# A new order of steps behind the start of the MLP, in a kernel of a DeltaNet block and an MLP block on one core

## The chip, the cores and the metric

The kernel runs on one core of one Trainium2 chip. The metric is the device time of one execution in microseconds (us); smaller is better. A run of the kernel before gave 519.6 us as the median of three (516.92 to 520.19).

The engines are named as in the profile: PE is TensorE (PEld its weight loads), DVE is VectorE, ACT is ScalarE, POOL is GpSimd and SP is SyncE, which here only issues DMAs. Each engine runs its instructions strictly in its own program order, and waits on semaphores for what other engines make.

## The reference, cut to what matters

The first block is the delta rule, a linear attention with a state of 48 x 48 for each of 4 x 8 heads, over 768 positions. The second is a layer norm without bias, two matrix products with a ReLU between them, and a residual.

```python
k_n = k / (np.linalg.norm(k, axis=-1, keepdims=True) + 1e-06)
for t in range(S):
    kt, vt, bt = (k_n[:, :, t], v[:, :, t], beta[:, :, t, None])
    y[:, :, t] = np.einsum('bhd,bhde->bhe', q[:, :, t], state)
    v_old = np.einsum('bhde,bhd->bhe', state, kt)
    state = state + bt[:, :, :, None] * np.einsum('bhd,bhe->bhde', kt, vt - v_old)
...
x = np.ascontiguousarray(attn_out.transpose(0, 2, 1, 3)).reshape(B, S, H * D)
xn = (x - mu) / np.sqrt(var + 1e-06) * g_ln
ch = np.maximum(xn @ w_ch1, 0.0) @ w_ch2
return (x + ch).astype(np.float32)
```

All is float32: q, k, v are (4, 8, 768, 48), w_ch1 is 384 x 1536 and w_ch2 is 1536 x 384.

## The kernel before, in words

**The recurrence in chunks.** The 768 positions are cut into 12 chunks of 64. Within a chunk the recurrence becomes products of matrices. For chunk c the steps have these names, which the later text uses:

- G (line 822): the gram product of the keys, 64 small matmuls ("a block"); ACT copies it to SBUF and SP sends it to DRAM and back in another layout.
- The inverse of a triangular matrix. For pairs of chunks `rows_inverse` (tags x1 to x5) does it row by row on DVE: 31 pairs of a product into `tmp` (line 910) and a subtraction from `xb` (line 917). Two short products e and z (lines 984 and 990) join the halves; chunk 1 has an extra pair (lines 947 and 952) around it.
- P (line 822, with the queries), ks and qs (line 1036, keys and queries against the state), u (lines 1055 and 1060 for chunk 1, line 1091 later), s (line 1108, the change of the state, which DVE adds to `s_all` in line 1118), y (line 1098, the chunk's output). Each is a block of 64 matmuls of 48 to 64 rows and columns.
- Between ks and u, DVE subtracts from v (line 1043). Behind y, ACT copies to `x`, DVE and ACT do the layer norm (lines 1142 to 1154), and the result is turned: by PE for the first three chunks (line 1188), by DVE and five DMAs on SP later (lines 1165 and following).

**The MLP by chunks.** `mlp(c)` runs for each chunk's 256 tokens. Chunk 0 has its own form (m0: first products in line 1410, second products in line 1452). Later chunks use a form of the second product with seven in place of eight block products (line 1527), whose combinations POOL makes (lines 1514 and 1552); from chunk 3 on the first product has fifteen block products (line 1311) with sums on POOL, DVE and ACT (lines 1271, 1294, 1334, 1329, 1338). Chunks 1 and 2 use line 1430.

**The weights** come as 64-bit words and are turned to float32 by a short chain for each of twelve pieces: ACT (lines 587 and 595), DVE (line 592), POOL (line 605).

**Keys and queries** of later chunks come into three buffers `tb` by eight DMAs each (`load_blocks`), the keys' from POOL's queue and the queries' from SP's, all issued in line 404; DVE turns each in one instruction (line 802).

**What sets the order.** Each piece of work is added to a list as a step with an engine, a function and the steps it depends on: 3,037 in all, numbered as they are added. `Line.emit` then runs the functions in the order that the string ORDER gives (numbers, ranges, and `f` for a filler matmul that keeps PE busy). So ORDER sets each engine's program order. `in_this_order` fixes it with dependencies that need no semaphore, and also ties the order of the DMAs of SP and ACT to each other. The synchronisation by data is put in by the framework, whatever the order is, with one exception in `emit`: a POOL step that is no DMA gets a semaphore wait for the last DVE step marked `port` that stands ahead of it in ORDER:

```python
if s.eng == "DVE" and s.plan.get("port"):
    shared = made[-1]
if s.eng == "Pool" and "bulk" not in s.plan and shared is not seen:
    tc.add_manual_dep(made[n], shared.name, ..., reason="shared port")
```

ORDER is written out by hand in the file; the costs that the steps carry (`dve(n)`, `act(n)`, `PASS`, due times in `DUE` and `CAP`) are not used when the kernel is built.

**Steps that the later text names**, with their numbers in ORDER:

| steps | what |
|---|---|
| 418, 420, 421 | chunk 1: the product of line 952 (`z` of its join), DVE's transpose of line 973, e1 |
| 437, 439, 438, 426 | chunk 1: ks1, DVE's subtraction from v, qs1, z1 |
| 440, 441, 443, 444, 445 | chunk 1: u in two halves, s1, DVE's sum into `s_all`, y1 |
| 480, 481 | x1: two small steps, on DVE and on POOL |
| 483 to 544 | x1: the 62 DVE instructions of its inverse |
| 658 to 665, 666, 667 | chunk 4: eight loads of keys from POOL's queue, DVE's turn (kt), G4 |
| 670 to 677, 678, 679 | chunk 5: the same, G5 |
| 375, 377; 381, 383; 387, 389; 393, 395 | pieces of w_ch2: DVE's conversion (line 592) and POOL's (line 605) |
| 396 | POOL: a memset ahead of loads of x1 |
| 572 to 617 | m0: first products on PE and ReLUs on ACT |
| 618 to 646 | m0: the last first product (618) and the second products |
| 787 to 795, 796 | chunk 2: loads of queries on SP, DVE's turn, P2 |
| 803, 805, 562 | s2, y2, e3 |
| 814, 867 | chunk 2: DVE's normalisation (line 1154); chunk 1's MLP: a combination on POOL (line 1514) |
| 924, 2140 | a load of keys on SP, for chunk 3 and for chunk 8 |
| 1199, 1201 | s4, y4 |

## Time and profile before

| what | value |
|---|---|
| time, median of three runs | 519.6 us (516.92 to 520.19) |
| span of the profiled execution, first to last instruction | 514.1 us |
| what the median has beyond that span | 5.5 us |
| PE busy | 493.1 us, 96% of the span |
| DVE busy | 353.5 us, 69% |
| POOL busy | 284.8 us, 55% |
| ACT busy | 206.9 us, 40% |
| granted PE clock | 0.999 of full speed |
| DMA, 16 queues, mean over the span | 106 GB/s |

The profile is of one execution, and gives its span; a device time of that same execution is not among the numbers, so the 5.5 us also hold what executions differ by. Busy times of PE are made of pipelined matmuls whose ends are modelled; the distance from one start to the next is the safer measure, and a step's "usual distance" below is its median over the steps of the same kind. A product of line 1527 is one matmul call and shows as two MATMUL records (the float32 passes), one of line 1311 as four, a block as 64. "issue" in the waits view is time in which an engine waited for nothing that the profile shows.

In the slices of the page PE is busy for nine tenths or more from the sixth slice on (about 64 us); before that, in the start that the change leaves as it is, PE waits more.

### The profile page before, as it was taken

To read this page: it belongs to the slowest core of one execution; us is meant where nothing else is said; L and a number is where in the kernel's file an instruction comes from. 1 tells how busy PE (TensorE), PEld (TensorE's weight loads), DVE (VectorE), ACT (ScalarE), POOL (GpSimd) and SP (SyncE) were. 2 spreads that over 40 slices of the span, in tenths; PEclk is the share of its full clock that TensorE was granted. 3 is DMA by queue.
4 is the path that set the end of the run, shared out by engine and by line. 5 is a ranking of instruction groups with operands and counts; after the bars stand their busy time and mean duration, and the time that the engine had idled before them with its cause. 6 is when DMAs were issued, how large, how long until landed. Compare 5 with 4: busy or idle time off the path is not lost.

```text
span 514.1 us, 22905 instructions
## 1 busy us (share of the span) xinstructions
PE 493.1 (96%) x10022; PEld 450.7 (88%) x10022; DVE 353.5 (69%) x816; ACT 206.9 (40%) x462; POOL 284.8 (55%) x447
## 2 busy tenths in 40 slices
PE   5897899999999999999999999999999999999997
PEld 3675797668888898999999999999999999999996
DVE  4688479899994999975997847898727346254241
ACT  4785764422533333351434343423514425324140
POOL 2634583144658879749477465283274551844644
PEclk9999999999999999999999999999999999999999
DMA  8958895577338755387454474313660321202011
GB/s 207 251 83 192 221 191 127 128 173 117 67 60 207 123 117 92 73 221 123 80 108 62 105 203 76 99 15 53 132 149 12 88 36 41 57 13 82 8 24 31
DMA packets 181635, 54.56 MB, mean 106 GB/s; under 512 B 164888, under 2 KB 177312, under 8 KB 181536
## 3 DMA queue, kind: packets, MB, share of 16 engines
q1 hardware_dynamic: 168512, 40.10, 37.4%
q10 hardware_dynamic: 10816, 9.83, 6.3%
q0 software_dynamic: 2208, 3.17, 4.3%
q8 instruction: 78, 1.28, 1.1%
q14 instruction: 21, 0.17, 0.1%
HBM read 36.30 MB, written 16.78 MB: 103 GB/s over the span
## 4 chain that ended last, share of the span: by engine, by line
PE 85%; DVE 5%; DMA 3%; issue 2%; ACT 1%; SPq 1%; POOL 1%; DVEq 0%; ACTq 0%; POOLq 0%
PE f L1527 28%; PE f L1311 24%; PE f L1430 6%; PE two L822 3%; PE f L1452 3%; DMA tb<-in_q_dram 2%; PE by L1098 2%; PE by L1036 2%; PE two L1091 2%; PE two L1036 2%; PE two L1108 2%; PE f L1605 1%; DVE xb L917 1%; SPq L404 1%; DMA kr<-in_k_dram 1%
## 5 line engine op out<-in xcount | busy, mean ns | idle before, releaser
L1527 PE MATMUL f<-w_sb,h_all 128*128 128x192 f32 x396 | 83.9, 330 | 0.0
L1514 POOL TENSOR_TENSOR h_all<-h_all 128x256 f32<-128x256 f32 x99 | 74.8, 767 | 9.4 <-PE f L1527 3.3
L1527 PE MATMUL f<-words,h_all 128*128 128x192 f32 x396 | 79.5, 329 | 0.2 <-POOL h_all L1514 0.2
L1552 POOL TENSOR_TENSOR words<-h_all 128x128 f32<-128x128 f32 x66 | 30.2, 478 | 74.4 <-ACT h_all L1338 50.2
L1334 DVE TENSOR_TENSOR h_all<-f,h_all 128x512 f32<-128x512 f32 x72 | 49.2, 686 | 30.5 <-PE f L1311 25.9
L1527 PEld LDWEIGHTS f<-w_sb,h_all 128*128 128x128 f32 x396 | 65.3, 190 | 1.6 <-POOL h_all L1514 0.2
L1527 PEld LDWEIGHTS f<-words,h_all 128*128 128x128 f32 x396 | 65.1, 190 | 1.6 <-POOL h_all L1514 1.0
L910 DVE TENSOR_TENSOR tmp<-xb,gb 128x31 f32<-128x31 f32 (+19 forms) x139 | 56.0, 403 | 3.7 <-POOL xb L897 0.5
L917 DVE TENSOR_TENSOR xb<-xb,tmp 128x31 f32<-128x31 f32 (+19 forms) x139 | 51.4, 370 | 2.5
L1329 ACT COPY h_all<-f 128x512 f32<-128x512 f32 x45 | 25.8, 586 | 62.9 <-PE f L1311 39.3
L404 POOL DMA_DIRECT2D tb<-in_k_dram x64 | 41.9, 658 | 8.2 <-PE f L631 7.1
L1338 ACT ACTIVATE h_all<-h_all 128x512 f32<-128x512 f32 x54 | 32.5, 626 | 30.0 <-DVE h_all L1334 29.8
L1311 PE MATMUL f<-x_new,w_sb 128*128 128x128 f32 x288 | 41.4, 278 | 0.0
L1311 PE MATMUL f<-xnt,w_sb 128*128 128x128 f32 x288 | 40.4, 278 | 0.1
L1311 PEld LDWEIGHTS f<-x_new,w_sb 128*128 128x128 f32 x288 | 37.4, 191 | 0.4
L1311 PEld LDWEIGHTS f<-xnt,w_sb 128*128 128x128 f32 x288 | 36.8, 191 | 0.5 <-issue 0.2
L1430 PE MATMUL f<-xnt,w_sb 128*128 128x256 f32 x144 | 33.9, 383 | 0.0
L1430 PEld LDWEIGHTS f<-xnt,w_sb 128*128 128x128 f32 x144 | 26.7, 190 | 3.5
L605 POOL TENSOR_TENSOR w_sb<-words 128x768 uint32<-128x768 uint32 (+1 forms) x11 | 15.3, 1400 | 23.7 <-issue 18.2
L1545 DVE TENSOR_TENSOR o<-f,x 128x192 f32<-128x192 f32 x33 | 11.2, 348 | 24.9 <-PE f L1527 17.2
L1136 ACT COPY x<-by 128x384 f32<-128x384 f32 x23 | 10.6, 481 | 42.6 <-DVE o L1545 27.2
L1527 PE MATMUL f<-w_sb,words 128*128 128x192 f32 x132 | 27.6, 332 | 0.0
(247 smaller groups left out, 1003.6 us busy)
## 6 DMA issues: line engine op xcount, KB each, us to landing
words<-in_moe_w_ch_dram ACTq DMA_DIRECT2D x20, 384.0 KB, 5.2
gd<-gsb SPq DMA_DIRECT2D x11, 512.0 KB, 4.1
v<-in_v_dram SPq DMA_DIRECT2D x24, 192.0 KB, 3.6
kr<-in_k_dram SPq DMA_DIRECT2D x46, 96.0 KB, 3.7
out_dram<-o SPq DMA_DIRECT2D x46, 96.0 KB, 2.5
xld<-xlt SPq DMA_DIRECT2D x9, 384.0 KB, 3.6
xnt<-xld SPq DMA_DIRECT2D x36, 96.0 KB, 3.0
tb<-in_q_dram SPq DMA_DIRECT2D x40, 64.0 KB, 3.5
```

The source lines that it names most:

```text
L404: add(eng, cost, lambda: QUEUE[eng].dma_start(out=out_, in_=in_), r, w, bulk=n * ns / 16e3, np=n, **kw)
L910: lambda j=j, n=n, w=w, t=t: nc.vector.tensor_tensor(out=t, in0=xv[:, 0:n, j : j + 1].to_broadcast([128, n, w]), in1=gv[:, j : j + 1, j + ...
L917: "DVE", dve(n * w), lambda t=t, rest=rest: nc.vector.tensor_tensor(out=rest, in0=rest, in1=t, op=ALU.subtract),
L1036: nc.tensor.matmul(dst[half(e), hp, j], src[drows(hp), (e if n else key_half(c, hp, e)) * GP + j], s_all[drows(hp), e, j], start=(n == 0 o ...
L1311: nc.tensor.matmul(wide(p[:, f : f + 128]), w[:, f : f + 128], r, start=start and i == 0, stop=True, skip_group_check=True)
L1329: add("ACT", act(512), lambda: nc.scalar.copy(o, p), pk, ok)
L1334: add("DVE", dve(512), lambda: nc.vector.tensor_tensor(out=o, in0=x, in1=y, op=op), [*xk_, *yk], ok)
L1338: add("ACT", act(512), lambda: nc.scalar.activation(o, o, ACTF.Relu, scale=scale), [], ok)
L1430: nc.tensor.matmul(p[:, 0:TOK], w1_sb[:, t, f * 128 : (f + 1) * 128], xnt[:, t], start=(t == 0), stop=(t == KC - 1))
L1514: add(eng, cost, lambda: e.tensor_tensor(out=out_, in0=x, in1=y, op=op), r, w, port=2 if eng == "Pool" else 1, pr=-2)
L1527: lambda f=f, t=start and f == order[0]: nc.tensor.matmul(p[:, 0:D2], lhs(f), rhs[:, f], start=t, stop=(f == order[-1]), skip_group_check=True
L1552: lambda f=f + i: e.tensor_tensor(out=s3[f], in0=one(0, 0)[0](f), in1=one(1, 0)[0](f), op=ALU.subtract),
```

## The change

Only the string ORDER changes (lines 131 to 248). The first 374 of its entries stay; the next 2,674 are the same steps in another order; the last 14 stay. On PE the first 50 steps are the same, up to s0, the state's first change, at 59.6 us; on DVE the first 128, on ACT 106, on POOL 39 and on SP 44. No step, instruction, buffer or dependency by data changes; the waits marked "shared port" follow from ORDER and so change with it.

The diff, cut to the stretches that the later text speaks of:

```diff
 ORDER = """
...
-250 345 349-350 576 578 406 362 577 579 301 407 321 333 432 431 309 307 302-303 308 304 473 306 305 471-472 474 788
-351 356 363 357 252 658 415 433-434 582 580 598 370 364 581 599 373 435 604 583 605 368 584 610 586 365 413 470 414
-611 585 588 416 372 587 475 590 401 787 790 792 789 791 793-794 589 379 417 591 378 592-596 616 600 374 597 602 601
-606 418 376 603 608 436 666 369 476-479 481-489 480 490-495 375 496-499 670 675 672 1073 674 677 377 371 676 500
-419-420 501 617 607 380 635 609 636 614 391 421 437 502-507 381 508 795 509 439 510-519 424 615 423 612 620 438 384
-390 382 425 422 426 429-430 428 427 637 621 440-441 638 385 392 442 639 445 394 386 447 443 520-523 444 524 393
-525-527 622-623 667 624 640 383 678 387 668 446 388 613 389 679-680 528 450 529 395 1085 625-626 618 530 451 448 455
-531 456 449 452 532 650 533 457 534 453-454 535-536 651 537 641 627 642-643 628-629 644 796 458 462 645 630 538 652
...
-559 711-713 655 714-715 692 716 561 717-728 562 801 863 841 846 802 864 805 854 856 866 927 843 857 855 936 729 565
-564 563 566 865 803 807 806 730 810 808 848-849 809 811 815 812 847 731 804 876-877 869-870 732 813 871 937 567 872
...
+578 576 356 362 359 432 431 306 304-305 303 473 307-308 302 472 474 471 787 363 357 415 579 364 577 252 582 580 598
+433-434 581 368 599 583 370 673 470 365 373 435 604 584 586 605 610 378 416 369 670 371 413-414 587 379 585 588 611
+372 475 417 589-590 924 788-790 792 794 791 793 784 591-594 596 418 595 597 602 600 616 601 603 608 380 376 617 609
+374 436 476-479 674 665 675 481-497 419-420 498-500 381 437 421 606 385 607 614 612 635-636 666 677 672 676 375 377
+423 425 613 422 424 390-391 439 480 678 501-521 426 438 615 620-621 637 429 428 427 622 382 430 440 384 441 623 618
+638-639 442 394 392 443 386 388 445 383 795 1073 393 395 466 444 522-525 387 667 640 446-448 450 449 451 668 452 389
+396 468 624-625 641 679-680 455 619 650 526-527 453 528-529 651 530-531 652 456 532 454 457 533-544 642-643 796
...
+558 557 560 840-841 860 713 655 561 714-722 657 723-731 801 861-863 846 864 843 802 865 467 856 927 857 866 936 805
+803 562 807 565 563 566 806 564 810 808 811 815 809 812 847 804 848-849 732 876-878 567 879 816 733 937 817 813 734
...
 3032-3034 3026 3035 3027 3036
 """
```

PE's part of the first stretch, read out of these lines with the names of the steps (f for a product of m0):

| order | PE from step 418 to G4 |
|---|---|
| before | z, f, f, f, f, e1, ks1, f, f, qs1, z1, f, f, u, u, f, f, y1, s1, f, f, G4 |
| after | z, f, f, f, f, ks1, e1, f, f, f, f, f, z1, qs1, f, f, f, f, u, u, f, f, f, f, s1, y1, G4 |

## The prediction

> **What bounds the kernel now.** I read the page's busy times first, then the waits of TensorE (PE) behind the start of the MLP, then the timeline where they lie.

> ```profile
> span 514.1 us, 22905 instructions
> ...
> PE 493.1 (96%) x10022; PEld 450.7 (88%) x10022; DVE 353.5 (69%) x816; ACT 206.9 (40%) x462; POOL 284.8 (55%) x447
> ...
> q8 instruction: 78, 1.28, 1.1%
> ```

> PE is the bound: 96% of the span. The waits view, PE alone, from 61 us (the new order begins on PE at 61.5 us) to the end, adds up to only 4.2 us:

> ```profile
> PE by L1036 <- issue: 1.3, 1, 1.3
> PE two L822 <- issue: 0.8, 2, 0.6
> PE two L1108 <- issue: 0.7, 1, 0.7
> PE two L1091 <- issue: 0.4, 1, 0.4
> PE two L1055 <- issue: 0.4, 1, 0.4
> PE f L1527 <- POOL h_all L1514: 0.2, 1, 0.2
> PE two L1036 <- issue: 0.2, 1, 0.2
> PE f L990 <- ACT es L996: 0.2, 1, 0.2
> ```

> Nearly all is "issue": PE stopped inside a block of 64 small matmuls and no semaphore ended it. Three of these stops in the timeline of PE:

> ```profile
> 87.02 0.95 PE L1036 MATMUL by<-s_all,qt 48*64 48x48 f32 x49 [1.26 <-issue]
> ...
> 91.03 0.56 PE L1055 MATMUL two<-v,xt 32*64 32x48 f32 x22 [0.36 <-issue]
> ...
> 102.84 0.32 PE L822 MATMUL two<-kt 48*64 48x64 f32 x2 [0.63 <-issue]
> ```

> The windows view counts the PE instructions between these stops:

> ```profile
> 87.02:91.03 4.01, 3.55 (x127) 2.45 (x128) 3.84 (x9) 2.25 (x5) 0.00 (x0) 1.00 0.40 123
> 91.03:102.84 11.81, 10.99 (x384) 7.92 (x383) 9.55 (x20) 5.29 (x8) 2.29 (x2) 1.00 0.54 125
> ```

> 127 + 128 = 255 and 384 + 383 = 767, three times 255.7. The page has 20,044 PE instructions in 78 packets of its instruction queue: 257 each. So the stops sit on packet ends: PE waits there for its next code. A block issues 128 instructions in about 1 us, so two blocks use up a packet in 2 us, while in these lines the next one came 4.01 us later.

> Start to start, the PE steps from 61.5 to the last one at 509.8 us take 448.3 us. Each step's usual distance to the next, summed, is 434.0: some 332 for the products of the MLP (462 of L1527 at 0.325, 270 of L1311 at 0.447, 24 of L1430 at 1.295, 46 of L1410 and L1452 at 0.67 and 0.645) and 102 for the blocks (0.68 to 1.09 each) with their changeovers. Some 76 short pauses of 0.105 make 8; 12 longer stops make 6.1 (5.3 on code, 0.8 on ACT or POOL). Of the 6.1, 3.8 lie between 87 and 104 us. This 6.1 is all that an order can win.

> **The change part by part.** The same 3,037 steps run; none is added or removed. Another step stands ahead of 657 of PE's 957, 460 of DVE's 816, 318 of ACT's 489, 352 of POOL's 443 and 259 of SP's 332.

> *PE's own work.* A changeover from a product to a block costs 0.093 (0.540 against 0.447), back some 0.11. The old order has 68 of each, the new 67. The sum of distances stays 434.0: 0, bounds -0.2 and +0.2.

> *The stretch from the product `z` of chunk 1 (step 418) to the gram block G4 (667).* Here DVE decides. DVE in the groups view, from the end of the transpose L973 (step 420) to the start of the state sum L1118 (step 444):

> ```profile
> L917 DVE TENSOR_TENSOR xb<-xb,tmp 128x240 f32<-128x240 f32 (+6 forms) x11 | 5.7, 517 | 0.3
> L910 DVE TENSOR_TENSOR tmp<-xb,gb 128x231 f32<-128x231 f32 (+6 forms) x12 | 4.9, 406 | 0.3
> L802 DVE STREAM_TRANSPOSE qt<-tb 128x1024 f32<-128x1024 f32 x1 | 1.2, 1239 | 0.0
> L1118 DVE TENSOR_TENSOR s_all<-s_all,two 128x768 f32<-128x768 f32 x1 | 1.0, 955 | 1.9 <-PE two L1108 1.9
> L1043 DVE TENSOR_TENSOR v<-v,two 128x768 f32<-128x768 f32 x1 | 0.9, 944 | 0.0
> L592 DVE TENSOR_SCALAR words<-words 128x768 uint32<-128x768 uint32 x1 | 0.6, 555 | 0.0
> ```

> 26 instructions, 13.3 us, then 1.9 idle for PE. The new order puts 32 there: two more transposes L802 (kt of chunks 4 and 5, steps 666 and 678: 2 x 1.24), two more conversions L592 (2 x 0.555), step 480 (0.2) and one more L917 (0.35): 13.3 + 4.1 = 17.4. PE gets five more products L1410 there (eight for three): its distances from 418 to G4 go from 17.0 to 17.0 + 5 x 0.67 - 0.15 = 20.2. From the start of 418 (78.00) to the end of L973 (81.41) it is 3.4 now. So G4 can start 3.4 + 17.4 + 0.95 (L1118) + 0.3 (now 97.97 - 97.66) = 22.1 behind 418, and PE is there after 20.2: it waits 1.9. With the shortest times of the inverse's 24 instructions it is 0.3, and with PE's two packet ends (below) still open ahead of it up to 3.8. I take 1.9, by the durations of the same instructions. In the old order the stretch and the one behind it cost the 3.8 named above; the new one has no packet used up in under 3.5 us from G4 to the end of the MLP's first chunk, and P2 comes 6.2 behind G4 instead of 10.1. Net -1.9, bounds 0 and -3.5.

> *DMAs and POOL here.* On POOL the loads of `tb` (665, 672 to 677; 0.66 of POOL each, landing after 3.0 to 3.5) now follow each other ahead of the conversion 377, so that kt 678 can stand early on DVE: they are issued behind step 481, some 5 us ahead of need. The memset 396 (0.95) goes from the first place on POOL to behind the conversion 389; its reader is a load near 117 us. On SP the load 924 of chunk 3 goes ahead of the eight loads of chunk 2 (0.62 later), and those of chunk 8 move up to 79 places. Adding SP's issues at 0.62 and the landings of the page's DMA list to each release, the least margin to the PE step served is 5.4 us (5.1 in the old order): 0. If that cover went, each place would cost PE 0.6.

> *Code supply behind 110 us.* From the packet ends found above I counted on, 255 PE instructions at a time. By distances, a packet is used up in under 3.5 us at eight places of the new order, twelve of the old. Behind 110 us the shortfall to 3.5 sums to 4.8 (old: 5.5); the longest are y2, s2, e3 in a row (1.8 us for a packet: 1.7) and y4, s4 (2.1: 1.4). The old order's 5.5 cost a measured 1.5. At that rate the new costs 1.3: -0.2, bounds -1.5 and +3.3 (the full 4.8). [...]

> *Handovers behind 110 us.* PE steps that wait for another engine: with row durations added along each, 16 of 357 have less than 0.15 us of cover in the old order, 26 in the new. The old 16 cost 0.8; 26 at that rate 1.3: +0.5, bounds -0.8 and +2. Adding each queue's instructions from their releases, DVE's worst lag behind its PE reader is 0.6 (old 2.2, at L1118 of chunk 6), POOL's 0.3 (old 0.4).

> *A shared port.* POOL steps wait for the last marked DVE step ahead of them in ORDER: 51 such waits behind the fork for 57. The tightest new one is the combination 867 of chunk 1 behind DVE's 814, with 0.2 us of cover: 0 to +0.5, taken as 0. Queued behind it are the other combinations of that MLP, and PE's products of L1527 wait for them.

> Sum: 0 - 1.9 - 0.2 + 0.5 = -1.6. The profiled span of 514.1 becomes 512.5. The median of the three runs, 519.6, stands 5.5 above the span, which I carry over: 518.0.

> **The rivals.**
> *1. No waits are left.* The order was placed so that all handovers meet: 519.6 - 6.1 = 513.5. For it: DVE's worst lag falls from 2.2 to 0.6. Against: 1.8 us for a packet at y2, s2, e3, and 17.4 us on DVE ahead of G4.
> *2. DVE is held by POOL ahead of G4.* In that stretch POOL runs three conversions L605 (377, 383, 395; mean 1.4 on the page) where the old order had two. If DVE stands still for each, G4 waits 4.2 more: 522.2. It is slower than before from 1.6 more. Against: now POOL is busy for 2.2 us in the stretch and DVE's idle time there, the wait for PE apart, is 0.6. [...]
> *3. Code arrives every 4.0 us all along,* as it did at 87 to 91 us. Then the packets behind 110 us lose 9.6 instead of 1.3: 518.0 + 8.3 = 526.3, slower. It decides from 3.6 us on (over 1% from 3.9). Against: by the same count the old order would have lost 11.6 there and lost 1.5; for: back-to-back blocks y2, s2, e3 are new.

> **How the numbers follow.** Forecast 0.52, rival 1 0.10, rival 2 0.20, rival 3 0.18. The likeliest alone reaches from 516.0 to 521.0. To leave out no more than 2 in 10 the range goes from 514.5 (most of rival 1 out) to 524.0 (rival 2 in, most of rival 3 out). About 1%, 5.2 us, is what a measurement of this kernel can tell from no change (the three runs spread over 516.92 to 520.19). Faster by more, under 514.4: 0.7 of rival 1, 0.07. Slower by more, over 524.8: 0.7 of rival 3 and a little of rival 2, 0.16. The rest, 0.77, is within 1%.

> **What would show it.** Right: PE's waits from 61 us on stay between 2 and 6 us; the 1.3 and 0.6 on "issue" at 87 and 103 us are gone; G4 follows L1118 and waits 1 to 3 us for it, DVE having no idle time ahead. Wrong: a stop of over 1.5 us on "issue" at y2, s2, e3 (near 135 us) or at y4, s4 (rival 3); POOL's L605 and DVE's L910 stretched beside each other ahead of G4 (rival 2); a wait for a DMA landing anywhere on PE (the SP margin was wrong); or a PE sum of distances that is not 434.

## The result, and the profile after

The new order is slower: 524.54 us, median of four runs (522.86 to 526.28), against 518.67 before (four runs, 516.92 to 520.19). The ratio is 1.011, 95% interval 1.008 to 1.015. The forecast was 518.0 with a range of 514.5 to 524.0: wrong in sign, and the median lies outside the range. In the later sessions before ran more often and its median was 516.6 to 516.9, so ratios, each against before's runs of the same session, are what to compare below. The ratios leave out two later executions that lay over 1.5% above the fastest of their kernel (523.28 of "new to 808, then old" and 525.45 of "new, loads spread" in the table of experiments).

The profiled execution of the new order took 522.86 us, span 521.1, against a span of 514.1. From its page:

```profile
span 521.1 us, 22880 instructions
...
PE 498.5 (96%) x10022; PEld 453.9 (87%) x10022; DVE 351.3 (67%) x816; ACT 207.3 (40%) x462; POOL 280.5 (54%) x447
...
PEclk9998998999999999999999999999999999999999
```

PE is the bound as it was, and the span is 7.0 us longer. In the clock row (tenths of full speed) slices 4 and 7 show 8: from 45.6 and from 79.75 us the clock was halved for 3.41 us each (granted 0.50 in both windows). The first lies in the common beginning, the second does not. The waits view of PE from 61 us to the end (line, what it waited for, us in all, times, longest):

```profile
PE by L948 <- issue: 1.6, 1, 1.6
PE f L1307 <- DVE h_all L1330: 0.9, 1, 0.9
PE f L1406 <- ACT h_all L1414: 0.9, 1, 0.9
PE f L1523 <- POOL h_all L1510: 0.7, 1, 0.7
PE by L1094 <- issue: 0.7, 1, 0.7
PE f L986 <- issue: 0.7, 2, 0.4
PE f L980 <- issue: 0.6, 1, 0.6
PE f L1523 <- DVE o L1541: 0.5, 1, 0.5
PE two L1051 <- issue: 0.4, 1, 0.4
PE by L1032 <- ACT xt L998: 0.2, 1, 0.2
```

(Lines are four lower than before's.) It sums to 7.2 us where before had 4.2, and what is new are waits for data: 3.2 us for DVE, ACT and POOL where before had 0.4.

To lay the whole out I use the prediction's measure: each PE step's distance to the next, less the usual distance of its kind. What is above counts as loss: waits, short pauses, and halved clock. I count from s0 (358), PE's last common step, to 832, the second PE step of chunk 1's MLP, and from there to PE's last step. Between two kernels a figure of loss is good to about 0.5:

| one profiled execution each | s0 to 832: usual + loss | 832 to the end: usual + loss |
|---|---|---|
| before | 51.8 + 6.2 | 383.0 + 9.3 |
| after | 50.2 + 8.4 | 384.2 + 14.4 |

The first part costs 0.6 more and the second 6.3 more, nearly all of the difference between the spans. The loss behind 832 grew by 5.1. Of that, waits over 0.13 us make 3.8 (6.1 against 2.3), and within these handovers of data 3.3 (4.1 against 0.8). Three of after's handovers (197.6, 223.6 and 419.0 us) make 2.5 of its 4.1.

Two places in the trace of after show how a part of it comes about. **Late place, 219 us.** DVE, then POOL, in the timeline (start, us, engine, line, operation, tiles, shape):

```profile
219.27 2.29 DVE L906 TENSOR_TENSOR tmp<-xb,gb 128x207 f32<-128x207 f32 x1
221.48 1.23 DVE L798 STREAM_TRANSPOSE kt<-tb 128x1024 f32<-128x1024 f32 x1
222.65 0.33 DVE L913 TENSOR_TENSOR xb<-xb,tmp 128x207 f32<-128x207 f32 x1
222.90 0.68 DVE L1330 TENSOR_TENSOR h_all<-f,h_all 128x512 f32<-128x512 f32 x1
```

```profile
218.91 0.66 POOL L400 DMA_DIRECT2D tb<-in_k_dram  x1
219.58 1.28 POOL L1267 TENSOR_TENSOR w_sb<-w_sb,qt 128x512 f32<-128x512 f32 x1
220.80 0.46 POOL L1290 TENSOR_TENSOR x_new<-x_new,xnt 128x128 f32<-128x128 f32 x1
221.22 0.79 POOL L1541 TENSOR_TENSOR o<-o,words 128x192 f32<-128x192 f32 x1
```

The product into `tmp` (step 1153) takes 2.29 us; in before the same step took 0.37:

```profile
216.59 0.37 DVE L910 TENSOR_TENSOR tmp<-xb,gb 128x207 f32<-128x207 f32 x1
```

In after it starts beside a POOL instruction, POOL's next two follow without a gap, and it ends 0.3 behind the end of L1290. Behind it on DVE stand a turn (1.23) and then L1330 (step 1265), whose input PE had finished at 218.7. PE waits for that sum until 223.63.

**Late place, 415 us.** POOL's timeline:

```profile
411.64 0.73 POOL L1510 TENSOR_TENSOR h_all<-h_all 128x256 f32<-128x256 f32 x1
414.62 1.48 POOL L681 TENSOR_TENSOR v<-v,kpair 128x768 f32<-128x768 f32 x1 [2.25 <-DMA v<-in_v_dram]
416.06 0.73 POOL L1510 TENSOR_TENSOR h_all<-h_all 128x256 f32<-128x256 f32 x1
```

POOL stands 2.25 us for a transfer: step 2720 scales v of chunk 11, and SP's load 2714 that it needs is issued at 410.98. In before it was issued at 381.64, and 2720 waited for nothing:

```profile
418.78 1.48 POOL L685 TENSOR_TENSOR v<-v,kpair 128x768 f32<-128x768 f32 x1
```

Its product is used by DVE at 445.1. The combinations L1510 for the running MLP stand behind it, and PE waits for one of them until 419.03. Six traces have the load at this place (one of them, shown below, carried into before), and PE's wait follows POOL's: POOL stood 1.2, 1.5, 2.3, 3.4, 3.8 and 7.1 us for v, and PE 0, 0, 0.7, 1.9, 2.2 and 6.8 for POOL.

**Early place, 66 to 79 us.** The chain of waits of after:

```profile
66.44 6.06 DMA gb<-gd
...
72.57 0.26 ACT nrm_b L882
72.83 0.49 ACT es L951
73.31 0.18 ACT h_all L1414
73.49 0.04 issue
73.53 2.27 PE f L1406 x18
75.81 0.67 PE by L948 x49
76.47 1.62 issue
```

A load takes 6.06 us to land (the new order issues four weight loads of ACT within 3.3 us there, where before spread them over 7; with the loads spread out, in an experiment below, it landed in 2.8), ACT waits for it, PE waits 0.9 for ACT, then stops 1.62 inside `z` for code, and the halved clock follows. This looked like the main cause. It was not, as the first two experiments show.

### The profile page after: what moved, and what is told of

It reads as the page before. It is cut to its first block, busy times and chain, and to the rows that moved or that the text cites. A ratio compares the mean times of both kernels' runs of the same rounds, so it can differ in the third digit from the quotient of the medians.

```text
span 521.1 us, 22880 instructions
## 1 busy us (share of the span) xinstructions
PE 498.5 (96%) x10022; PEld 453.9 (87%) x10022; DVE 351.3 (67%) x816; ACT 207.3 (40%) x462; POOL 280.5 (54%) x447
## 3 DMA queue, kind: packets, MB, share of 16 engines
q8 instruction: 78, 1.28, 1.0%
## 4 chain that ended last, share of the span: by engine, by line
PE 75%; DVE 6%; DMA 6%; SPq 4%; ACT 4%; issue 3%; POOL 1%; DVEq 0%; ACTq 0%; POOLq 0%
PE f L1523 27%; PE f L1307 20%; SPq L400 4%; PE f L1426 3%; PE two L818 3%; PE f L1448 3%; PE two L1032 2%; PE by L1094 2%; PE f L1406 2%; PE by L1032 2%; PE two L1087 1%; DMA tb<-in_q_dram 1%; DMA gb<-gd 1%; DMA xld<-xlt 1%; ACT xt L728 1%
## 5 line engine op out<-in xcount | busy, mean ns | idle before, releaser
L1510 POOL TENSOR_TENSOR h_all<-h_all 128x256 f32<-128x256 f32 x99 | 73.2, 750 | 19.9 <-PE f L1523 9.8
L1523 PE MATMUL f<-w_sb,h_all 128*128 128x192 f32 x396 | 81.6, 330 | 0.0
L1548 POOL TENSOR_TENSOR words<-h_all 128x128 f32<-128x128 f32 x66 | 29.0, 457 | 78.9 <-ACT h_all L1334 38.6
L1330 DVE TENSOR_TENSOR h_all<-f,h_all 128x512 f32<-128x512 f32 x72 | 49.0, 685 | 30.7 <-PE f L1307 24.2
L1541 DVE TENSOR_TENSOR o<-f,x 128x192 f32<-128x192 f32 x33 | 11.3, 352 | 38.1 <-PE f L1523 28.1
```

The costliest lines, as they stand in the source:

```text
L1330: add("DVE", dve(512), lambda: nc.vector.tensor_tensor(out=o, in0=x, in1=y, op=op), [*xk_, *yk], ok)
L1510: add(eng, cost, lambda: e.tensor_tensor(out=out_, in0=x, in1=y, op=op), r, w, port=2 if eng == "Pool" else 1, pr=-2)
L1523: lambda f=f, t=start and f == order[0]: nc.tensor.matmul(p[:, 0:D2], lhs(f), rhs[:, f], start=t, stop=(f == order[-1]), skip_group_check=True
L1548: lambda f=f + i: e.tensor_tensor(out=s3[f], in0=one(0, 0)[0](f), in1=one(1, 0)[0](f), op=ALU.subtract),
```

## The experiments

Theories at the start: **1**, the early burst of loads; **2**, thinly covered handovers in the later part; from the second group on theory **3**, a special case of 2: a queue works in order, so an instruction that waits for a transfer, or that DVE or POOL holds up for the other, stops all that stands behind it; and **4**, the supply of code. Ratios are against before. Edits of ORDER are shown as the order on one engine's queue.

The losses are of one profiled execution each, which can lie far from its kernel's median: 527.77 for a median of 522.05 in the third row, the slowest of its six.

| kernel | ratio, 95% interval | loss s0 to 832 | loss behind 832 |
|---|---|---|---|
| after | 1.0111 (1.0076 to 1.0146) | 8.4 | 14.4 |
| new to 808, then old | 0.9997 (0.9973 to 1.0020) | 6.4 | 9.3 |
| old to 808, then new | 1.0108 (1.0065 to 1.0152) | 6.3 | 17.0 |
| new, loads spread | 1.0076 (1.0040 to 1.0112) | 5.4 | 14.7 |
| new, nrm_b later | 1.0095 (1.0059 to 1.0131) | 5.8 | 13.8 |
| new, four moves | 1.0071 (1.0041 to 1.0102) | 7.9 | 11.3 |
| before, two moves | 1.0197 (1.0161 to 1.0233) | 6.2 | 19.6 |
| new, packets shifted | 1.0178 (1.0139 to 1.0216) | 8.3 | 12.3 |
| new, ten moves | 1.0047 (1.0015 to 1.0080) | 3.8 | 13.2 |
| new, ten moves, e3 apart | 1.0068 (1.0041 to 1.0095) | 5.5 | 11.7 |
| loads spread, then old | 0.9989 (0.9970 to 1.0008) | 4.8 | 10.9 |
| the same, mended | 0.9976 (0.9947 to 1.0004) | 6.3 | 9.3 |

**Halves exchanged.** The first 808 entries of the one order (to about 120 us), then the remaining steps in the other's sequence.

```diff
-ORDER = new
+ORDER = new[:808] + [s for s in old if s not in new[:808]]
```

> The new order up to its 808th entry (about 120 us, the start of the second chunk's MLP), then all remaining steps in the order of before. In the two profiles PE's stops above usual distance sum to 13.0 us in the new order (7.0 of it from 60 to 104 us, 6.1 behind) against 6.1 (3.8 and 2.3). Theory 1, the early burst of loads: most of the loss arises ahead of 104 us and stays with this kernel: 3 to 4 us over before (ratio 1.006 to 1.008), with ACT's nrm_b waiting over 2 us for gb, a stop on issue of over 1 us near 78 us and a stretch of half clock of 3.4 us behind it. Theory 2, thinly covered handovers in the later part of the new order: this kernel is within 1 us of before (0.998 to 1.002).

```diff
-ORDER = new
+ORDER = old[:808] + [s for s in new if s not in old[:808]]
```

> The order of before up to its 808th entry, then the remaining steps in the new order. Theory 1, the early burst of loads: no wait of ACT for gb over 1 us, no half clock between 60 and 500 us, and only the later part's 3.8 us over before are left or less: ratio 1.002 to 1.007. Theory 2, the later handovers: all of the loss stays: 5 to 6 us over before (1.010 to 1.012). With the kernel above, the two differences against before should sum to about that of the whole new order (5.9 us).

Measured 0.9997 and 1.0108. Theory 1 fell: with the new beginning alone the time is before's, although its trace has the same stop (1.89 us near 78 us): it loses 6.4 us ahead of 832 where before loses 6.2. All of the slowdown comes with the later part, whose loss is 9.3 with the old sequence and 14 to 17 with the new; and the two differences sum to 1.05% where the whole new order has 1.11%. One point of theory 1's failed too: the clock was halved behind 420 us in the second kernel's trace (mean granted 0.990), which it had excluded.

**Loads spread, and ACT's step later.** In the first, of the queues of ACT and SP, 378, 379 and 401, 784, 924 go back:

```diff
-ACT: 378 ... 379 585 ... 589      SP: 401 early, 784 and 924 with the loads of m0
+ACT: 585 ... 589 379 591 378      SP: 401 behind 788, 784 and 924 ahead of 785
```

> The new order with five loads spread out as before had them: two of ACT's four weight loads issued 4 to 5 us later, the row load beta_b behind the loads of gb and tb, and the loads of v and kr for later chunks back to about 100 us. Theory 1: gb lands within 4 us, ACT's nrm_b does not wait over 1 us, PE's waits of 1.0 at 73.5 us and 1.8 at 78.8 us and the half clock behind them go: 3 to 4 us below the new order (ratio against before 1.003 to 1.006). Theory 2: no change against the new order (1.010 to 1.012).

```diff
-ACT: 475 417 589 591
+ACT: 417 589 591 475
```

> The new order with one step of ACT moved: nrm_b, which waited 2.6 us for gb, behind the two hidden-layer products that it held up. The loads stay bunched. Theory 1: PE's wait of 1.0 for h_all at 73.5 us goes, gb still takes 6 us to land, and the stop on issue near 78 us stays or moves by a few tenths, as does the half clock: 0.5 to 1.5 us below the new order (ratio against before 1.008 to 1.010); if the stop of 1.8 and the half clock go as well, they hung on ACT's lag and not on the loads of code, and the ratio is 1.003 to 1.005. Theory 2: no change against the new order.

Measured 1.0076 and 1.0095, whose intervals hold the new order's 1.0111: on time, neither theory is told apart. In the traces, the loss of the beginning is 5.8 to 8.4 in the five kernels with bunched loads (mean 7.4) and 3.8 to 6.3 in the five with spread loads (mean 5.2). So by these means the burst costs the beginning some 2 us, though the two ranges overlap and no run shows it on time; it is not what made the kernel slower. Moving `nrm_b` alone took away PE's wait for ACT and left the stop for code (2.3) and the halved clock (24 matmuls of L1406 behind the stop took 4.16 us, 3.08 where the clock was full).

**Four moves behind 180 us.**

```diff
-DVE: 1134 1135 1136 1137 1026 1380     DVE: 1153 1566 1154 1265
+DVE: 1134 1026 1135 1136 1137 1380     DVE: 1265 1153 1566 1154
-DVE: 1319 1665                         SP: 2319 2714 2724
+DVE: 1665 1319                         SP: 2715 2714 ... 2319 2724
```

> The new order with four steps moved, all behind 180 us: DVE's output sum 1026 of chunk 2 ahead of three steps of the inverse; DVE's hidden sum 1265 of chunk 3 ahead of the product 1153 that POOL held for 1.9 us; DVE's output sum 1319, which waits for output transfers, behind the turn of the queries 1665 (as before had it); and SP's load 2714 of v for chunk 11 back to where before had it, behind 2715. Theory 3, in-order queues (DVE and POOL are stopped by a transfer or by the other's use of their common port, and the PE step that has to wait stands behind): PE's waits near 198, 224, 231 to 240 and 419 us go; in the four traces of the later part they summed to 2.5, 5.1, 4.8 and 1.7, so 2.5 to 4.5 us off the new order, ratio against before 1.002 to 1.006. Rival, that stops for code and half clock make the loss: no change, 1.009 to 1.012.

Measured 1.0071, between the two expectations: 0.4% below the new order, where theory 3 had 0.5 to 0.9%, and the two intervals overlap, so that time alone does not show a gain. The trace is plainer. Its waits of PE from 105 us on:

```profile
PE f L1523 <- POOL h_all L1510: 0.8, 1, 0.8
PE by L980 <- issue: 0.4, 1, 0.4
PE f L1523 <- DVE h_all L1330: 0.2, 1, 0.2
PE by L1032 <- ACT xt L998: 0.2, 1, 0.2
```

The waits near 224, 231 to 240 and 419 us are gone, and the loss behind 832 is 11.3, against 15.0 as the mean of the four traces of the new later part without a shift of packets. The first line is new: at 196.8 us PE waits for a combination behind POOL's 1224, which waits for the marked DVE step 1137, ahead of which my first move had put 0.35 us of work. A wait took the place of the one removed.

**Two of these places put into before.**

```diff
-SP: 2715 2137 2714 2134                 POOL: 2486 2720 2600    DVE: 1665 1319
+SP: 2715 2137 2134 ... 2385 2714 2725   POOL: 2458 2720 2455    DVE: 1319 1665
```

> The order of before with two places as the new order has them: SP's load 2714 of v for chunk 11 directly ahead of POOL's conversion 2720 and both among the combinations of chunk 8's MLP; and DVE's output sum 1319 ahead of the turn 1665. Theory 3: POOL stands 1.5 to 4 us for the landing of v near 410 us, PE waits 0 to 2.3 for h_all behind it, and where the output transfers land late 0.8 to 1.2 at P6: on the mean 1 to 2.5 us slower than before, ratio 1.002 to 1.005. Rival: the old order has cover for both, PE's waits there stay under 0.2 and the ratio is 0.998 to 1.002.

Measured 1.0197, 10 us: theory 3's sign, four times its price. PE's two longest waits and POOL's longest in this kernel (lines one lower than before's):

```profile
PE f L1526 <- POOL h_all L1513: 7.1, 2, 6.8
PE two L821 <- DVE qt L801: 1.3, 1, 1.3
```

```profile
POOL v L684 <- DMA v<-in_v_dram: 7.1, 1, 7.1
```

On SP the load 2714 now stood behind transfers that could not start before 409.7, was issued at 412.4 and landed at 416.3. POOL waited 7.1 us for it and PE 6.8 for POOL; the clock was halved for 6.83 us from 419.3 on (12 matmuls of L1526 then took 4.21, against 2.15 for 12 of L1527 in before at the full clock), which makes most of the remaining 3. Three steps moved at two places cost more than the whole new order.

**The price of code by itself.** P6 in before, 13 times in a row.

```diff
+                for _ in range(12 if s is self.steps[1666] else 0):
+                    s.fn()
                 s.fn()
```

> The kernel before with the block P6 (64 small matmuls, the same product into the same buffer) issued 12 more times in a row: 1,536 more PE instructions, 6.0 packets of 255.7, 13.1 us by the usual distance of 1.09. If a packet of code takes 4.0 us to come whatever else goes on (rival 3 of the prediction), the row takes about 24 us and PE shows stops on issue of 1.8 at each packet end behind the first; if 3.5 us, 21 us and stops of 1.3; if code is fetched ahead without limit, 13 to 14 us and no stop over 0.3.

The row in PE's timeline (lines two higher than before's):

```profile
229.73 2.10 PE L824 MATMUL two<-qt,kt 48*64 48x64 f32 x128
232.22 2.10 PE L824 MATMUL two<-qt,kt 48*64 48x64 f32 x128 [0.40 <-issue]
236.23 2.65 PE L824 MATMUL two<-qt,kt 48*64 48x64 f32 x128 [1.91 <-issue]
240.50 3.69 PE L824 MATMUL two<-qt,kt 48*64 48x64 f32 x128 [1.62 <-issue]
244.78 9.44 PE L824 MATMUL two<-qt,kt 48*64 48x64 f32 x320 [0.58 <-issue]
```

It takes 24.4 us for 14.2. Of the 10.2 more, 4.5 are stops, one every 128 matmuls (256 instructions) up to 244.78. The other 5.7 are the matmuls themselves: the clock was halved from 237.5 us on, for 20.48 (granted 0.65 in the window from 236.23 to 240.50 and 0.50 from there to the end of the row), and 320 of them then took 9.44, or 3.8 for 256 instructions. So the total of 24, which rival 3 of the prediction gives, came out in part by luck, as the last 320 lost nothing to code that can be seen. The period did come out where PE stood for code: from one stop's end to the next it is 4.01, 4.27 and 4.28 us. (The instruction queue's packets start at 229.82, 233.32, 238.00, 242.33, 245.90, 249.92 and 253.38, 3.93 apart on the mean, but the last three distances lie where PE's own pace was 3.8.) The first crossing costs 0.40 only, the next two 1.91 and 1.62: by my reading of these rows one packet is fetched ahead, and only a second one used up quickly costs the rest.

**Packets shifted.** Each of the 25 fillers divided into four, which issues 150 more PE instructions ahead of s0.

```diff
-nc.tensor.matmul(f_[0][:, 256:512], nought, nought[:, 0:1].to_broadcast([128, 256]))
+for n in range(4):
+    nc.tensor.matmul(f_[0][:, 256 + 64 * n : 320 + 64 * n], nought, nought[:, 0:1].to_broadcast([128, 64]))
```

> The new order with each of the 25 filler matmuls of 256 columns divided into four of 64: 150 more PE instructions ahead of 60 us, nothing else. Theory 4, the stops on issue sit on packet ends: the stop of 1.6 to 2.8 us that all three new beginnings have between step 418 and the first products behind it (near 78 us) moves by 105 or 150 instructions or goes, and those at z2, e3 and z3 change place. Rival: the stop stays between 418 and the next product, so it hangs on data. On time I expect within 2 us of the new order (ratio against before 1.007 to 1.015).

The stop inside `z` (L948) moved from PE instruction 3,242 to 3,498, a packet later and 106 instructions further on in the program; those at z2, e3 and z3 were gone, and new ones stood at 93 and 97 us:

```profile
83.28 0.94 PE L948 MATMUL by<-xt,es 32*32 32x32 f32 x87 [1.09 <-issue]
87.83 0.91 PE L1032 MATMUL two<-s_all,kt 48*64 48x48 f32 x47 [0.19 <-issue]
93.20 0.27 PE L1406 MATMUL f<-xnt,w_sb 128*128 128x128 f32 x1 [1.69 <-issue]
97.20 0.32 PE L1032 MATMUL by<-s_all,qt 48*64 48x48 f32 x5 [0.70 <-issue]
```

The rival's sign, a stop between 418 and the next product, is there as well, since `z` is 418; but the stop moved by 106 instructions inside it, to a number 256 higher, as theory 4 has it. So the stops sit at fixed instruction numbers, whatever the program does there. On time I missed (1.0178): s0 started 5.6 us later than in after, which is the divided fillers' cost, and from s0 on the profiled execution was 2.2 us shorter.

**All mended, and e3 apart.** The four moves, the five loads spread, and POOL's 1224 behind 1035; then besides PE's e3 (562) away from y2 and s2.

```diff
-POOL: 1018 1224 1019 1035 1225
+POOL: 1018 1019 1035 1224 1225
```

> The new order with the five loads spread out ahead of 110 us (as in the run of that name), the four moves behind 180 us, and one more: POOL's product 1224 behind the combination 1035, since in the run with four moves PE waited 0.8 at 196.8 us for a combination that stood behind it. What PE loses above its usual distances is counted from 832, the first PE step of chunk 1's MLP, to the end: 9.3 in the order of before, 14.4, 17.0, 14.7 and 13.8 in four runs of the new later part, 11.3 with four moves. Theory 3 (in-order queues): 10.0 to 10.9 with ten. Ahead of 832, 4.7 with the loads spread against 5.1 before, with 1.1 less of usual distance (partly a shift between the two stretches). Sum: minus 1 to plus 1 us against before, ratio 0.998 to 1.003. Rival, that something in the later part stays which these traces do not show: 1.004 to 1.008, as with four moves.

```diff
-PE: 840 860 801 861 862 863 846 864 805 803 562 848
+PE: 840 860 801 861 862 562 863 846 864 805 803 848
```

> The kernel of the ten moves with PE's block e3 (step 562) moved from directly behind y2 and s2 to behind the product 862, nine PE steps earlier, near where before had it. In the run of the ten moves PE lost 0.85 and 0.70 us on issue at e3 and z3, in four others of the new later part 0 to 1.5 in the two. Theory 4 (code: y2, s2 and e3 in a row use up a packet of 255 instructions in 1.8 us, and packets came every 3.9 us in the row of 13 blocks): the stop at e3 goes, that at z3 goes or shrinks, 0.8 to 1.5 us less behind step 832, ratio 1.002 to 1.004 against the 1.0047 of the ten moves. Rival, that the stop only moves to another packet end: the sum of stops on issue from 125 to 150 us stays over 1.2 us and the ratio 1.004 to 1.006.

Ten moves gave 1.0047, which is the rival's range (1.004 to 1.008) and not theory 3's (0.998 to 1.003): 1.5 us came back at e3 and z3 as stops for code, and the loss behind 832 was 13.2, where theory 3 had 10.0 to 10.9. The wait of 0.48 for DVE's output sum 1026 was gone, but PE now waited 0.48 for a later one at 203.2 us, which stands behind a turn of the keys (1.23): once more a wait in the place of the one removed. With e3 apart these stops are gone; the waits of PE from 105 us on name no stop on issue:

```profile
PE f L1523 <- DVE o L1541: 0.5, 1, 0.5
PE f L1426 <- DVE words L1541: 0.4, 1, 0.4
PE f L1523 <- DVE h_all L1330: 0.2, 1, 0.2
PE by L1032 <- ACT xt L998: 0.2, 1, 0.2
PE f L1307 <- DVE o L1541: 0.2, 1, 0.2
```

The loss behind 832 fell to 11.7, as theory 4 has it, but the time did not: 1.0068, outside both expectations and not told apart from 1.0047. The new later part never came down to the old one's 9.3. Taken together, the four kernels with the new later part as it was (without the shifted packets) have ratios of 1.0076 to 1.0111, mean 1.0098, and the three with the moves 1.0047 to 1.0071, mean 1.0062: the moved places are worth about a third of the slowdown, and the other two thirds stay. What is left in this trace are waits of 0.1 to 0.6 at ten places (2.9) and 1.8 more than before in pauses under 0.13 us.

**A version to use.** The new beginning with its loads spread, the old later part; then besides SP's 1850 behind 1571, and DVE's 2501 ahead of 2729 (which is where the new order has it).

> The new order up to its 808th entry with the five loads spread out, then the order of before. Ahead of step 832 the loss is that of the run with the loads spread, 4.7 (before: 5.1), at 48.7 of usual distance; behind it that of before, 9.3 at 383.7. From the first step to the last that is 446.4 against 448.3 before: 1.5 to 2 us faster, ratio 0.996 to 0.998, if the loads were what held the beginning. If the loss at the beginning does not hang on them, 6 to 7.6 there as in the runs with the loads bunched: 0.999 to 1.003.

```diff
-SP: 1573 1850 1574 1572 1571      DVE: 2493 2729 2501
+SP: 1573 1574 1572 1571 1850      DVE: 2493 2501 2729
```

> The kernel with the spread beginning and the order of before behind it, with two more moves: SP's load 1850 behind the load 1571 of gb, and DVE's output sum 2501 ahead of the turn 2729, as the new order has it. In its run PE waited 0.77 at 237 us (gb landed late) and 0.48 at 419 us (the turn waited for its queries); in three other runs of that later part 0 to 0.8 at each. If those transfers hold PE, both waits go and it is 0.5 to 1.2 us faster, ratio 0.996 to 0.998 against before; if others come late in their place, 0.998 to 1.000 as it was.

Measured 0.9989 and 0.9976, with medians of 516.80 against 516.61 and 515.56 against 516.93. The first lies between its two expectations (the beginning lost 4.8 as forecast, the later part 10.9 for 9.3), the second inside the first of its two. Both intervals hold no change; the second is the fastest of all and 1.2 us below before by the point, no more than that.

## Why the prediction was wrong, point by point

**PE's own work: 0.** Right. The usual distances from s0 to the end sum to 434.8 before and 434.4 after.

**The stretch from 418 to G4: -1.9 (0 to -3.5).** Not there. With the new beginning alone the ratio was 0.9997 (0.9973 to 1.0020), so at most 1.4 us were won. The step that failed is "here DVE decides". DVE's 32 instructions between the transpose and its sum into `s_all` took 16.1 us for the 17.4 forecast, but 18.5 passed from 81.52 to 100.03: DVE stood 1.3 for ACT's conversions (L583) and 0.9 for PE's s1, where I had no idle time. PE was late by itself. On the way it had lost 3.6: 1.6 to a stop for code inside `z`, 1.6 to the halved clock and 0.4 at a later packet end; and the last stop ahead of G4, 0.7 inside y1, was for code too. The point estimate took no packet end ahead of G4 to cost anything (two stood in its bounds); the dearest of them stood inside step 418 itself.

**DMAs and POOL here: 0, with a least margin of 5.4 us.** This step failed in its rule, and with it the sentence on SP. I measured each landing against the PE step that the load serves. For the load 2714 that margin is some 35 us: issued at 411, its product first needed on PE at 449.9. What counted was who stands behind the instruction that waits for it: the combinations of the running MLP on POOL. PE lost 0 to 2.3 us there in five traces, 7.0 when the place was carried into before, and nothing in the three kernels with the load back in its place. In the same way DVE's 1319 waited 5.6 us for an output transfer in the trace with the loads spread, with the turn 1665 behind it, and P6 lost 0.8. The price of a lost cover, which I gave as 0.6 a place, was too low as well: here it was the rest of the landing, for which POOL stood 1.2 to 7.1 us.

**Handovers behind 110 us: +0.5 (-0.8 to +2).** This is the term that was mis-sized most: +3.3 in the profiled pair. I had counted 26 thin places and priced them at their mean of 0.05. Most of the loss sits in four places (three of them in this pair, 2.5 us), and each was late because a step ahead of it on its queue was held up.

**A shared port: 0.** What rival 2 supposed, DVE held beside POOL, does show, but not where I put it. Ahead of G4 in after DVE had no stretched step over 0.5 us; at 219 us one was held for 1.9 (2.29 us in after, 0.37 in before), in all five traces in which the order of the later part was the new one at that place, and PE lost 1.1 each time. With the sum 1265 moved ahead of it, PE lost at most 0.2 there. The rows of after show step 1153 beside POOL's: it begins 0.31 ahead of L1267 and ends 0.3 behind the end of L1290. That a port common to the two engines held it, as the kernel's reason for its waits and theory 3 have it, no run shows. The new order has less of such stretching in all, 18.9 us on DVE against 24.8 (above each step's shortest time in six traces); it is the place behind it that costs.

**Code behind 110 us: -0.2 (-1.5 to +3.3), and rival 3.** The places were named (y2, s2, e3 in a row), and the period was right (4.0 to 4.3 us where PE stands for code; the 3.5 to which I counted the shortfall was my own, and no run showed it). In six traces with this sequence z2, e3 and z3 lost 0 to 2.2, 1.1 on the mean; five with the old sequence lost 0.4 to 1.0 between 125 and 157 us, 0.7 on the mean. That is +0.4 and not the +8.3 of rival 3, as would follow from one packet held ready, my reading of P6's rows.

**The carry-over of 5.5 us** between the profiled execution and the median was wrong: in nearly all runs the time stands 1.7 to 2.2 us above the span, and the profiled execution of before was one of the fastest (13 of before's 85 later runs have a shorter span than 514.1). With 1.7 the forecast would have been 514.2, further off.

**What stays open.** By the traces, the kernel of ten moves with e3 apart is 1.4 us longer than before from s0 on; by its runs it is 3.5 us slower (2.1 to 4.9). Its runs that were only timed take some 2 us more than the profiled execution, which was the fastest of the twelve and had the full clock (1.000, mean of the twelve 0.995), and no trace shows where. A halved clock does not explain the slowdown: the runs of before have a mean clock of 0.994 to 0.995 in each later session, those of the kernels with the loads spread, four moves, ten moves and e3 apart 0.994 to 0.996, and all four are slower by 0.5 to 0.8%. So of the new order's 1.1% about two thirds have no cause shown, only a place, the later part. Of the 1.8 us in pauses under 0.13 us the cause wasn't sought.

## What to carry to other kernels

A load's margin is counted twice: to the step that it serves, and to whatever stands behind the instruction that will wait for it on its own engine; here the first was 35 us and the second nothing. Before moving a wait in an in-order queue, list the next five instructions of that queue and when the bounding engine needs them. And when a trace shows one striking chain of waits, exchange the halves of the change before believing it: here the striking chain was worth nothing on balance. Quiet places of about one microsecond were worth more, and mending them still gave back only about a third.
